# An adaptive-layer-norm block with windowed attention: w_mod's first third in two groups of feature columns, with the first Q weights between them

## The chip, the cores and the metric

The kernel runs on one core of one Trainium2 chip. The metric is the device time of one execution in microseconds, the median of several runs. The kernel before takes 323.13 us (three runs, 322.71 to 323.54).

## The reference, cut to what matters

`x` has 2048 rows of 640 features in bf16. Six modulation vectors of 640 come from one row `c` and `w_mod` (640 x 3840). The first third of `w_mod`'s columns gives `sa` and `ca`, with which the first layer norm's output is shifted and scaled before the QKV projection.

```python
mod = (_silu(c) @ w_mod).reshape(c.shape[0], 6, 1, -1)
sa, ca, ga, sb, cb, gb = ...
h = _layernorm(x, axis=-1) * (1 + ca) + sa
x = x + ga * _A_ref(h, A_wqkv, A_wo)        # 32 heads of 20, causal window of 256
h = _layernorm(x, axis=-1) * (1 + cb) + sb
x = x + gb * _B_ref(h, B_w_gate, B_w_up, B_w_down)   # (sigmoid(g) * u) @ w_down, F = 1536
```

## The kernel before

The 2048 rows are worked through in 8 chunks `a` of 256 rows, each two blocks `bi` of 128. For each chunk: layer norm (`ln1`, `ln_stats`), turning the normalized rows so that features lie on partitions (`hT`, five feature tiles `dt` of 128, called `kt` where they are summed over), modulation of `hT` by the columns `scA` and `shA`, projection to Q, K and V (`qkv`), attention (`score_set`, exponentials on ScalarE, masks on GpSimd, `burst` for the product with V, `norm`), output projection and MLP. TensorE works on chunks ahead: the projections of chunk a + 2 are issued before attention of chunk a.

**The order of work** is not decided at run time. `Prog.op` collects 2139 operations with their reads and writes; the list `PRIO` gives each a number. Sorted by it, the numbers give the order; the number modulo 5 names the engine (PE, ACT, DVE, POOL, SP). `schedule` only chooses buffers and semaphores along that order; `emit` writes each engine's instructions in it, with a wait wherever a read or write depends on another engine. So each engine works through its own list strictly, and a step whose input is late holds up all behind it on that engine. SP issues nearly all DMAs, in the order of its list, and they share one queue.

**The start** is what the change touches. Before anything can be projected, the modulation of layer norm one has to be known, so these come first:

- SP issues x block 0 (`load_x`), then w_mod's first third as six DMAs with an x block between: four by `load_bulk` (line 642), each one row tile `kt` of 128 rows x 1280 columns (320 KiB, runs of 2560 bytes), and the fifth row tile in two halves (lines 644 to 646). They lie for now in the space of `wd`. Then come wqkv's columns in pieces of 320 (`load_w3`, line 636, 400 KiB each, runs of 640 bytes): the first half of Q (`wq`), half of K, x blocks 2 and 3, the other half of K, V (640 columns), and the other half of Q.
- TensorE meanwhile runs six pairs of dummy products (`warm`, line 672), turns c, and seeds the sums with a product of the identity and a tile of ones (line 749), which adds the 1 of `1 + ca`.
- For each row tile of w_mod that has landed, TensorE runs ten products of 128x128 weights by a 128x64 tile of silu(c) repeated (`fnA`): five column groups `cg` of 128 for `ca` (bank 1) and five for `sa` (bank 0), summed over the five row tiles in two banks of `psA`. Behind the first three stand two padding products each (`pad`, line 682, from `FILL`).
- When all are summed, one VectorE copy (line 764) takes the ten columns to `mA`, whose halves are `shA` and `scA`.
- `pe_transposes` turns chunk 0: TensorE multiplies the normalized blocks by the identity (tag `aptr0`), three feature tiles in one bank and two in another; ScalarE or VectorE copies them to `hT` (line 838). Then ten modulations in place, one for each feature tile and block (lines 847 and 848), each of which waits for `R_mA`, that is for the whole copy.
- `qkv(0)` projects, 320 columns at a time, with five products over `kt` each. In the table before, the first Q columns of both blocks come first, then K's first. Their results go to `stg` (line 908 on ScalarE, 909 on VectorE), are turned by TensorE (`qtr0`) and copied to `QT` and `KT`. The first scores (`score0`) need these; two exponentials (line 1019) follow each score.

Lines 672, 682, 692 and 693 are helpers through which all of TensorE's products go. From chunk 1 on, the modulation is part of the copy (line 872/873) or follows a DMA transpose (line 815).

Of the kernel before, what the change touches and what calls it, by code (L numbers as in the profile page):

```python
# [361 lines left out]
def c_pe(n):  # L362
# [132 lines left out]
MW = 64  # L495
LEAD = 2
NE = 5
EW = 48 * 64
EDGE = 2
DEDGE = 0.245  # L500
FILL = (2, 2, 2, 0, 0)
WSE = (("dve", "pool"), ("dve", "pool"))
QMAX = 4.5
PAIR = 0
PAIRO = 0
XHP = ((2, 0), (3, 0), (4, 0), (4, 1), (5, 0), (5, 1))
OWE = lambda a: "sp"
# [3 lines left out]
def build(nc, A_x, A_wqkv, A_wo, B_x, B_w_gate, B_w_up, B_w_down, c, w_mod, out, S=2048):  # L511
# [61 lines left out]
    def R(name):  # L573
        return Res(name)
# [61 lines left out]
    def load_w3(lo, hi, work, prio, tag, **kw):  # L636
        dma(lambda: wqkv[:, :, lo:hi], lambda: wqkv_src[:, :, lo:hi], work, writes=R_w3[lo // 160:hi // 160], prio=prio, tag=tag, **kw)
# [653 lines left out]
```

## Time and profile before

| | before |
|---|---|
| median of 3 runs | 323.13 us (322.71 to 323.54) |
| profiled execution, its own time | 323.24 us |
| its span, first to last instruction | 321.5 us |
| granted TensorE clock | 1.000 |
| instructions | 11632 |
| DMA moved in the span | 37.85 MB |

The profile is one execution. Engines are PE (TensorE's products), PEld (its weight loads), DVE (VectorE), ACT (ScalarE), POOL (GpSimd) and SP, which only issues DMAs here. A busy time counts instructions only, not waits. An arrow back from a group or a row names what ended the wait before it. A row of the timeline has start, length, engine, line, operation and how many instructions were merged. A product's length contains the time in which it drains, so products that follow one another overlap: their pitch is what they cost.

### The profile page before, as it was taken

What the parts mean: (1) busy time and instruction counts of PE and PEld (TensorE: products, weight loads), DVE (VectorE), ACT (ScalarE), POOL (GpSimd) and SP (SyncE); (2) the same over time, 40 slices, a digit from 0 to 9 for tenths busy, and PEclk for the clock granted to TensorE, in tenths of its full rate; (3) what the DMA queues carried; (4) which work ended last, traced back from release to release, by engine and by line L of the source; (5) the groups of instructions that cost most, each with busy time, mean ns of one, the idle gap of its engine ahead of it and who ended that gap; (6) DMA issues with size and microseconds to landing.
All of it is one profiled execution on the core that took longest, in us unless ns stands there. A gap on an engine that the chain in (4) does not pass through costs nothing.

```text
span 321.5 us, 11632 instructions
## 1 busy us (share of the span) xinstructions
PE 316.9 (99%) x4877; PEld 223.9 (70%) x4877; DVE 209.7 (65%) x429; ACT 213.0 (66%) x315; POOL 178.4 (55%) x271
## 2 busy tenths in 40 slices
PE   8899999999999999999999999999999999999997
PEld 3565655557876677757776667887887788887885
DVE  4699997768779788764668457557472775454332
ACT  3599997989796869778867686877585753211120
POOL 4157987977666776887466576755647373002100
DMA  6999988899591728734027482240023112203101
GB/s 214 372 349 351 275 161 149 183 123 281 174 194 49 116 84 132 95 61 114 7 65 105 92 155 68 56 90 12 2 68 90 46 41 63 80 25 63 41 2 61
DMA packets 71182, 37.85 MB, mean 118 GB/s; under 512 B 45274, under 2 KB 69338, under 8 KB 71130
## 3 DMA queue, kind: packets, MB, share of 16 engines
q1 hardware_dynamic: 69968, 35.80, 48.3%
q10 hardware_dynamic: 1162, 1.31, 1.2%
q8 instruction: 38, 0.62, 0.9%
q14 instruction: 14, 0.11, 0.1%
HBM read 21.30 MB, written 5.25 MB: 83 GB/s over the span
## 4 chain that ended last, share of the span: by engine, by line
PE 96%; DMA 2%; SPq 1%; issue 0%; DVE 0%
PE M L692 80%; PE S L693 8%; PE M L693 7%; DMA wqkv<-in_A_wqkv_dram 2%; SPq L588 1%; DVE x L1215 0%
## 5 line engine op out<-in xcount | busy, mean ns | idle before, releaser
L1019 ACT ACTIVATE E<-S 128x512 bf16<-128x512 f32 (+2 forms) x184 | 150.7, 878 | 41.5 <-PE S L693 38.1
L1044 POOL TENSOR_SCALAR_AFFINE_SELECT E<-E 128x512 bf16<-128x512 bf16 (+1 forms) x176 | 139.5, 819 | 55.1 <-ACT E L1019 28.1
L692 PE MATMUL M<-wqkv,hT 128*128 128x480 bf16 (+1 forms) x340 | 73.6, 355 | 0.8 <-DMA wqkv<-in_A_wqkv_dram 0.8
L692 PE MATMUL M<-h2T,wu 128*128 128x256 bf16 x480 | 65.2, 273 | 0.0
L692 PE MATMUL M<-h2T,wg 128*128 128x256 bf16 x480 | 64.4, 273 | 0.0
L1196 DVE SCALAR_TENSOR_TENSOR hh<-sig,M 128x512 bf16<-128x512 f32 x48 | 32.7, 682 | 43.3 <-ACT sig L1194 32.4
L692 PE MATMUL M<-wd,hh 128*128 128x320 bf16 (+2 forms) x396 | 56.1, 295 | 0.0
L1194 ACT ACTIVATE sig<-M 128x512 f32<-128x512 f32 x48 | 28.8, 603 | 36.8 <-PE M L692 35.6
L692 PEld LDWEIGHTS M<-h2T,wg 128*128 128x128 bf16 x480 | 46.2, 98 | 6.9
L692 PEld LDWEIGHTS M<-h2T,wu 128*128 128x128 bf16 x480 | 45.3, 98 | 7.5 <-ACT E L1019 0.3
L692 PEld LDWEIGHTS M<-wqkv,hT 128*128 128x128 bf16 x340 | 30.3, 98 | 27.0 <-DMA wqkv<-in_A_wqkv_dram 0.9
L692 PEld LDWEIGHTS M<-wd,hh 128*128 128x128 bf16 x396 | 37.0, 98 | 15.0 <-issue 0.3
L693 PEld LDWEIGHTS S<-QT,KT 20*64 20x64 bf16 (+1 forms) x1856 | 19.9, 100 | 19.7 <-ACT E L1019 8.4
L693 PE MATMUL S<-QT,KT 20*64 20x256 bf16 (+5 forms) x1856 | 32.1, 228 | 0.0
L1215 DVE TENSOR_TENSOR x<-M,x 128x320 bf16<-128x320 f32 (+2 forms) x33 | 15.5, 475 | 23.1 <-PE M L692 22.7
L778 DVE BATCH_NORM_STATS2 st<-x 128x6 f32<-128x320 bf16 x64 | 28.7, 477 | 2.6 <-DMA x<-in_A_x_dram 2.1
L784 POOL TENSOR_SCALAR st<-st 128x2 f32<-128x2 f32 (+1 forms) x17 | 3.9, 229 | 42.3 <-DVE st L780 40.4
L1088 DVE STREAM_TRANSPOSE T<-M 128x512 f32<-128x512 f32 x32 | 21.6, 697 | 7.2 <-PE M L693 7.0
L692 PE MATMUL M<-wo,oT 128*128 128x320 bf16 x160 | 25.6, 300 | 0.0
L1149 DVE TENSOR_TENSOR x<-M,x 128x320 bf16<-128x320 f32 x32 | 15.5, 487 | 11.3 <-PE M L692 10.5
L693 PE MATMUL M<-E,V 128*32 128x128 bf16 (+1 forms) x960 | 22.8, 246 | 0.0
L693 PEld LDWEIGHTS M<-E,V 128*32 128x32 bf16 x960 | 19.1, 97 | 3.8 <-issue 1.7
(77 smaller groups left out, 239.1 us busy)
## 6 DMA issues: line engine op xcount, KB each, us to landing
x<-in_A_x_dram SPq DMA_DIRECT2D x24, 160.0 KB
doc<-On SPq DMA_DIRECT2D x64, 40.0 KB
wd<-in_B_w_down_dram SPq DMA_DIRECT2D x4, 480.0 KB
wqkv<-in_A_wqkv_dram SPq DMA_DIRECT2D x4, 400.0 KB
wu<-in_w_mod_dram SPq DMA_DIRECT2D x5, 320.0 KB
oT<-doc SPq DMA_DIRECT2D x8, 192.0 KB
out_dram<-x SPq DMA_DIRECT2D x9, 160.0 KB
wd<-in_w_mod_dram SPq DMA_DIRECT2D x4, 320.0 KB
```

Source lines behind the costliest of these rows:

```text
L588: return e.dma_start(dst(), src())
L692: return e.matmul(o, l, r, start=st, stop=sp, skip_group_check=True)
L693: return e.matmul(o, l, r, start=st, stop=sp, tile_position=tp, skip_group_check=True)
L778: A("dve", lambda e, g, bi=bi, j=j: e.bn_stats(v(bi * 12 + j * 6, 6), src[bi].ap[:, j * 320:(j + 1) * 320]), 0.48, reads=[src[bi].r()], wr ...
L784: A("pool", lambda e, g, lo=lo, hi=hi: e.tensor_scalar(v(28 + lo, hi - lo), var()[:, lo:hi], EPS, None, op0=ALU.add), 0.2, reads=[st.r(("m ...
L1019: A("act", lambda e, eng: e.activation(dst(), src(), ACT.Exp, scale=SM_SCALE), c_act(n), reads=[Sp.r()], writes=[E.r(key)], prio=3, tag=f" ...
L1044: A("pool", lambda e, eng: e.affine_select(rows(dst), rows(src), pattern=[[0, 8], [sign, n]], compare_op=ALU.is_ge, fill=0.0, base=base, c ...
L1088: A("dve", lambda e, g, h=h: e.transpose(T1.ap[:, 512 * h:512 * h + 512], X[h].ap), 0.694, reads=[X[h].r()], writes=[T1.r(h)], prio=3.5, t ...
L1149: A("dve", lambda e, g, ps=ps, bi=bi, half=half: e.tensor_tensor(x1[bi].ap[:, half * 320:half * 320 + 320], ps.ap[:, 0:320], x1[bi].ap[:, ...
L1194: A("act", lambda e, g, pg=pg, sg=sg: e.activation(sg.ap[:], pg.ap[:], ACT.Tanh, scale=0.5), c_act(512), reads=[pg.r()], writes=[sg.r()], ...
L1196: A("dve", lambda e, g, pu=pu, sg=sg, f0=f0: e.scalar_tensor_tensor(out=hh.ap[:, f0:f0 + 2, :], in0=sg.ap[:].rearrange("p (a b) -> p a b", ...
L1215: A("dve", lambda e, g, ps=ps, bi=bi, c0=c0, n=n: e.tensor_tensor(x1[bi].ap[:, c0:c0 + n], ps.ap[:, 0:n], x1[bi].ap[:, c0:c0 + n], op=ALU. ...
```

## The change

w_mod's first third is loaded, multiplied and copied in two groups of feature columns. Group A is feature tiles 0 to 2 (`SPL = 3`): 384 columns for `sa` and 384 for `ca`, in five DMAs, one for each row tile (192 KiB, runs of 768 bytes). Group B is feature tiles 3 and 4: 256 columns each, in three DMAs (row tiles 0 to 3 for `ca`, the same for `sa`, and row tile 4 for both; 256, 256 and 128 KiB, runs of 512 bytes). The first piece of Q's weights is cut in two: rows of feature tiles 0 to 2 (240 KiB) and of 3 and 4 (160 KiB).

```diff
-    load_bulk(wm_ap[0][:, 0:4, :], wm_src[:, 0:4, 0:1280], Rm[0][0:4], 1.1, 0.2, "wm0", cuts=(1, 2, 3, 4), lat=0.8)
...
+    SPL = 3
+    parts = [(0, SPL, kt, kt + 1, (1, 0)) for kt in range(NDT)] + [(SPL, NDT, 0, 4, (1,)), (SPL, NDT, 0, 4, (0,)), (SPL, NDT, 4, 5, (1, 0))]
...
+    for i, q in enumerate(parts):
+        c0, c1, k0, k1, banks = q
+        dma(lambda q=q: part(wm_ap[0], *q), lambda q=q: part(wm_src, *q),
+            0.11 * len(banks) * (c1 - c0) * (k1 - k0), writes=[R_part[i]], prio=0.2 + 0.01 * i, tag="wmA" if c0 == 0 else "wmB", lat=0.8)
...
-        load_w3(320 * i, 320 * i + 320, 1.05, 0.30 + 0.005 * i, "wq" if i < 2 else "wk", lat=0.9)
+        load_w3(320 * i, 320 * i + 320, 1.05, 0.30 + 0.005 * i, "wq" if i < 2 else "wk", parts=((0, SPL), (SPL, NDT)) if i == 0 else ((0, NDT),), lat=0.9)
...
+    for k, n in ((0, SPL), (1, NDT - SPL)):
+        psA_one.append(A("pe", lambda e, g, k=k, n=n: mm(e, psA.ap[:, k, 0:2 * n * MW], ident[:], Eall[:, 1, (SPL - n) * MW:(SPL + n) * MW], True, False), 0.16,
+                         reads=[R_one, R_ident], writes=[psA.r(k > 0)], prio=0, lat=0.2, tag="one", ni=2))
...
+    for i, (c0, c1, k0, k1, banks) in enumerate(parts):
+        def fnA(e, g, c0=c0, c1=c1, k0=k0, k1=k1, banks=banks):
+            for kt in range(k0, k1):
+                for bank in banks:
+                    for cg in range(c0, c1):
+                        ins = mm(e, place(c0, bank, cg),
+                                 wm_ap[0][:, kt, bank * D + cg * 128:bank * D + cg * 128 + 128], silubc[:, kt, 0:MW],
+                                 False, kt == NDT - 1)
+            return pad(e, FILL[k0]) if c0 == 0 and FILL[k0] else ins
...
+    for c0, c1 in ((0, SPL), (SPL, NDT)):
+        A("dve", lambda e, g, c0=c0, c1=c1: e.tensor_copy(mA[:, :, c0:c1], psA.ap[:, c0 > 0, 0:2 * (c1 - c0) * MW].rearrange("p (b a m) -> p b a m", b=2, m=MW)[:, :, :, 0]), 0.18,
+          reads=[psA.r(c0 > 0)], writes=[R_mA[c0 > 0]], prio=0, tag=f"fac{c0}")
...
-                    A(MOE, mo, {"dve": 0.24, "act": 0.48, "pool": 0.45}, port=True, reads=[dst.r(("t", dt, bi))] + Rmod,
+                    A(MOE, mo, {"dve": 0.24, "act": 0.48, "pool": 0.45}, port=True, reads=[dst.r(("t", dt, bi)), Rmod[dt >= SPL]],
...
-FILL = (2, 2, 2, 0, 0)
+FILL = (2, 1, 0, 0, 0)
```

Each group is seeded by a product of its own, with a tile of zeros (for `sa`) beside ones (for `ca`), and has its own bank. There are two copies to `mA`, and a modulation of chunk 0 waits only for the copy that holds its feature tile; `R_w3` likewise says of each Q piece which rows have landed. `PRIO` is a new table of 2147 numbers. In the start it reads, engine by engine:

- SP: x0, group A's row tile 2, x1, row tiles 1, 0, 4, 3, Q's first weights (rows of tiles 0 to 2), group B (`ca`, row tile 4, `sa`), Q's rest, K's first half, x3, x2, and on as before but for some pieces of w_mod's second third and x blocks.
- TensorE: group A's products, with the turning of block 0 among them and of block 1 behind, B's `ca` products, Q of block 0 over tile 0, then over tiles 1 and 2, B's `sa` products and row tile 4, Q of block 1 over tiles 0 to 2, then Q of both blocks over tiles 3 and 4, then K. In K, block 0's five products stand together, then a turn of Q, then block 1's.
- VectorE: both layer-norm statistics before both normalizations; the first copy, five modulations, the second copy, four modulations. POOL does the tenth; ScalarE none (two before). Three of the later evacuations change between ScalarE and VectorE.

From about 22 us on, every engine's list is the same as before.

More of the change, by code (lines that the diff above doesn't have):

```diff
@@ L574, in R @@
         return Res(name)
-    R_w3 = [R(f"wqkv{i}") for i in range(12)]
+    R_w3 = [[R(f"wqkv{i}a"), R(f"wqkv{i}b")] for i in range(12)]
     R_crow, R_ident, R_ccol, R_cth, R_siluc, R_silubc, R_wo = (R(n) for n in ("crow", "ident", "ccol", "cth", "siluc", "silubc", "wo"))
@@ L634, in build, with load_w3 @@
     wqkv_src = A_wqkv.rearrange("(t p) f -> p t f", p=128)
-    def load_w3(lo, hi, work, prio, tag, **kw):
-        dma(lambda: wqkv[:, :, lo:hi], lambda: wqkv_src[:, :, lo:hi], work, writes=R_w3[lo // 160:hi // 160], prio=prio, tag=tag, **kw)
+    def load_w3(lo, hi, work, prio, tag, parts=((0, NDT),), **kw):
+        for t0, t1 in parts:
+            dma(lambda t0=t0, t1=t1: wqkv[:, t0:t1, lo:hi], lambda t0=t0, t1=t1: wqkv_src[:, t0:t1, lo:hi], work * (t1 - t0) / NDT,
+                writes=[r for rs in R_w3[lo // 160:hi // 160] for r, t in zip(rs, (0, SPL)) if t0 <= t < t1], prio=prio, tag=tag, **kw)
     x0 = {}
@@ L747, in build @@
     R_one = R("one")
-    A("pool", lambda e, g: e.memset(Eall[:, 1, 0:5 * MW], 1.0), 0.3, writes=[R_one], prio=0)
-    p_E.init[1].append(A("pe", lambda e, g: mm(e, psA.ap[:, 1, 0:5 * MW], ident[:], Eall[:, 1, 0:5 * MW], True, False), 0.14,
-                         reads=[R_one, R_ident], writes=[psA.r()], prio=0, lat=0.2, tag="modA", ni=2))
+    A("pool", lambda e, g: e.memset(Eall[:, 1, 0:SPL * MW], 0.0), 0.25, writes=[R_one], prio=0, tag="ones")
+    A("pool", lambda e, g: e.memset(Eall[:, 1, SPL * MW:2 * SPL * MW], 1.0), 0.25, writes=[R_one], prio=0, tag="ones")
@@ new lines, in place @@
+    def place(c0, bank, cg):
+        at = bank * (SPL if c0 == 0 else NDT - SPL) * MW + (cg - c0) * MW
+        return psA.ap[:, c0 > 0, at:at + MW]
+    psA_one = []
+    for k, n in ((0, SPL), (1, NDT - SPL)):
+        psA_one.append(A("pe", lambda e, g, k=k, n=n: mm(e, psA.ap[:, k, 0:2 * n * MW], ident[:], Eall[:, 1, (SPL - n) * MW:(SPL + n) * MW], True, False), 0.16,
+                         reads=[R_one, R_ident], writes=[psA.r(k > 0)], prio=0, lat=0.2, tag="one", ni=2))
+    p_E.init[1].extend(psA_one)
@@ L751, in build @@
     oA = []
     fills = []
-    for kt, banks in [(kt, (1, 0)) for kt in range(NDT - 1)] + [(NDT - 1, (1,)), (NDT - 1, (0,))]:
-        def fnA(e, g, kt=kt, banks=banks):
-            for bank in banks:
-                for cg in range(5):
-                    ins = mm(e, psA.ap[:, bank, cg * MW:cg * MW + MW],
-                             wm_ap[0][:, kt, bank * D + cg * 128:bank * D + cg * 128 + 128], silubc[:, kt, 0:MW],
-                             kt == 0 and cg == 0 and bank == 0, kt == NDT - 1)
-            return pad(e, FILL[kt]) if FILL[kt] else ins
-        oA.append(A("pe", fnA, MW / 2400.0 * 5 * len(banks) + 0.2154 * FILL[kt], reads=[Rm[0][kt] if kt < NDT - 1 else R_half[banks[0]], R_silubc],
-                    writes=[psA.r()], prio=0, lat=0.2, tag="modA", ni=10 * len(banks) + 2 * FILL[kt], extra=wprev))
+    for i, (c0, c1, k0, k1, banks) in enumerate(parts):
[7 more added lines that the diff above has]
+            return pad(e, FILL[k0]) if c0 == 0 and FILL[k0] else ins
+        nf = FILL[k0] if c0 == 0 else 0
+        np = len(banks) * (c1 - c0) * (k1 - k0)
+        oA.append(A("pe", fnA, MW / 2400.0 * np + 0.2154 * nf, reads=[R_part[i], R_silubc],
+                    writes=[psA.r(c0 > 0)], prio=0, lat=0.2, tag="modA" if c0 == 0 else "modB", ni=2 * np + 2 * nf, extra=wprev + [psA_one[c0 > 0]]))
@@ L898, in ln1 @@
         if a < NPH:
-            turned[a] = pe_transposes(src, t, scA, shA, [R_mA], 1, a)
+            turned[a] = pe_transposes(src, t, scA, shA, R_mA, 1, a)
         else:
@@ L936, in qkv @@
             name = "q" if lo < D else "k" if lo < 2 * D else "v"
-            pe_chain(ps, wid, pairs, [R_w3[lo // 160:hi // 160] + [hT[a].r((kt, bi))] for kt in range(NDT)], prio, f"proj{name}{a}", hold=hold, first=a == 0 and hi <= 2 * D)
+            pe_chain(ps, wid, pairs, [[rs[kt >= SPL] for rs in R_w3[lo // 160:hi // 160]] + [hT[a].r((kt, bi))] for kt in range(NDT)], prio, f"proj{name}{a}", hold=hold, first=a == 0 and hi <= 2 * D)
             m = min(hi, 2 * D)
```

15 lines of the change are left out of this document (7 added, 8 removed), and 225 rows, old and new, of the table PRIO.

## The prediction

> **What bounds the kernel now.** I read the page first (busy time by engine, then the chain that ended last), then the chain in order of time, then the first 25 us in the timeline and in windows of 1 us. From the page:
>
> ```profile
> span 321.5 us, 11632 instructions
> PE 316.9 (99%) x4877; PEld 223.9 (70%) x4877; DVE 209.7 (65%) x429; ACT 213.0 (66%) x315; POOL 178.4 (55%) x271
> PE 96%; DMA 2%; SPq 1%; issue 0%; DVE 0%
> ```
>
> TensorE is busy 316.9 of 321.5 us and carries 96% of the chain. All it could win back is 4.6 us, part of which is the start and the last store. The 2% of DMA is one piece, at the head of the chain in order of time. The list of waits has it too, and two windows place it:
>
> ```profile
> 4.76 6.30 DMA wqkv<-in_A_wqkv_dram
> PE M L692 <- DMA wqkv<-in_A_wqkv_dram: 0.8, 1, 0.8
> 10.29:11.10 0.81, 0.00 (x0) 0.00 (x0) 0.70 (x5) 0.57 (x3) 0.00 (x0) 1.00 1.13 377
> 11.10:13.10 2.00, 1.99 (x13) 0.97 (x14) 1.82 (x9) 0.90 (x3) 0.00 (x0) 1.00 1.11 374
> ```
>
> In a window row the first column is the length, then the busy time of PE, PEld, DVE, ACT and POOL, the granted clock, the DMA share and GB/s. So the first Q weights land at 4.76 + 6.30 = 11.06 us, TensorE is empty from 10.29 to 11.10, and from there it is full. DMA runs at full stretch in that gap (377 GB/s): the start is bound by bytes. The change therefore matters by when the first projection ends and what stands behind it. The rest of the kernel only moves with that point.
>
> The stages of the start, from the timeline (start, length, engine, line; xN merges N):
>
> ```profile
> 2.17 2.54 SPq L588 DMA_DIRECT2D wd<-in_w_mod_dram  x5
> 4.76 1.42 SPq L588 DMA_DIRECT2D wqkv<-in_A_wqkv_dram  x2
> 7.88 3.38 SPq L588 DMA_DIRECT2D wqkv<-in_A_wqkv_dram  x3
> 7.04 0.46 PE L692 MATMUL S<-silubc,wd 128*128 128x64 bf16 x10
> 8.78 0.60 PE L682 MATMUL S<-E 128*128 128x512 bf16 x2
> 9.07 0.47 PEld L692 LDWEIGHTS S<-silubc,wd 128*128 128x128 bf16 x10 [0.20 <-DMA wd<-in_w_mod_dram]
> 9.78 0.51 PE L692 MATMUL S<-silubc,wd 128*128 128x64 bf16 x10
> 10.34 0.16 DVE L764 COPY mA<-S 128x10 f32<-128x10 f32 x1
> 10.60 0.88 ACT L847 ACTIVATE hT<-hT,mA 128x128 bf16<-128x128 bf16 x2 [0.24 <-DVE mA L764]
> 10.61 1.87 DVE L848 TENSOR_SCALAR hT<-hT,mA 128x128 bf16<-128x128 bf16 x8
> 11.11 2.69 PE L692 MATMUL M<-wqkv,hT 128*128 128x320 bf16 x16 [0.82 <-DMA wqkv<-in_A_wqkv_dram]
> ```
>
> Read downwards: w_mod's products, the copy to `mA`, ten modulations of `hT`, then projections. The last modulation ends at 10.61 + 1.87 = 12.48, so the first ten Q products are held by the modulations almost as much as by the weights. Of the 16 products in the last row ten are Q's and six K's; I call the first of K's K0. When K0 starts follows from the pitch of products that wait for nothing:
>
> ```profile
> 14.42 1.11 PE L692 MATMUL M<-wqkv,hT 128*128 128x320 bf16 x7
> L692 PE MATMUL M<-wqkv,hT 128*128 128x320 bf16 x16 | 2.7, 300 | 0.8 <-DMA wqkv<-in_A_wqkv_dram 0.8
> 13.63 0.95 PE L692 MATMUL M<-ident,stg 128*128 128x128 bf16 x12
> 12.35 0.44 ACT L908 ACTIVATE stg<-M 128x320 bf16<-128x320 f32 x1 [0.88 <-PE M L692]
> 14.06 0.60 ACT L908 ACTIVATE QT<-M 128x512 bf16<-128x512 f32 x1
> 15.47 0.40 PE L693 MATMUL S<-QT,KT 20*128 20x256 bf16 x8
> 15.92 1.94 ACT L1019 ACTIVATE E<-S 128x1024 bf16<-128x1024 f32 x2 [0.32 <-PE S L693]
> 18.36 1.94 ACT L1019 ACTIVATE E<-S 128x1024 bf16<-128x1024 f32 x2
> 20.44 0.40 PE L693 MATMUL S<-QT,KT 20*128 20x128 bf16 x16
> ```
>
> Seven products take 1.11 us and one 0.30, so the pitch is (1.11 - 0.30)/6 = 0.135. K0 starts six products before the end of the row of 16: 13.80 - 0.30 - 5 x 0.135 = 12.82. Twelve transposes take 0.95 with their waits. From 15.47 to 20.44 it goes score, two exponentials (1.94), score, two exponentials (1.94, to 20.30), score: there ScalarE sets the pace, and when the first score starts decides when TensorE gets through this stretch.
>
> **The change part by part.** The order tables, old and new, give each engine's order. From about 22 us on all five are the same as before (the last 878 of 929 TensorE steps, 387 of 429 VectorE, 307 of 323 ScalarE), so all that can move the time lies in the start.
>
> *Bytes.* The amount is unchanged; the order is not. Before: x block 0 and 1 (320 KiB), w_mod (1600), wq's first 320 columns (400): w_mod ends at 1920 KiB, the weights at 2320. After: both x blocks and group A (960, together 1280), wq's rows 0 to 383 (240, at 1520), group B (640, at 2160), wq's rest (160, at 2320), then K's first 400 (2720). So the first weights come 800 KiB earlier in the stream, but the last byte of w_mod comes 240 KiB later. Rates, by windows of 1 us:
>
> ```profile
> 3.00:4.00 1.00, 1.00 (x4) 0.38 (x4) 0.87 (x3) 0.00 (x0) 0.00 (x0) 1.00 1.12 328
> 4.00:5.00 1.00, 1.00 (x4) 0.45 (x3) 0.26 (x3) 0.21 (x1) 0.57 (x2) 1.00 0.76 246
> 5.00:6.00 1.00, 1.00 (x3) 0.30 (x2) 0.72 (x3) 0.16 (x1) 0.46 (x2) 1.00 0.76 207
> 6.00:7.00 1.00, 1.00 (x9) 0.63 (x8) 0.97 (x4) 0.40 (x2) 0.28 (x2) 1.00 0.82 291
> 7.00:8.00 1.00, 1.00 (x22) 0.72 (x21) 0.40 (x3) 0.68 (x2) 0.74 (x2) 1.00 0.99 375
> 9.00:10.00 1.00, 1.00 (x23) 0.88 (x22) 0.13 (x1) 0.02 (x1) 0.00 (x0) 1.00 1.12 362
> 17.00:18.00 1.00, 1.00 (x14) 0.58 (x15) 1.00 (x3) 0.88 (x2) 1.00 (x7) 1.00 1.04 401
> ```
>
> The wait that ended at 9.07 is for w_mod's fourth row tile, 1600 KiB into the stream; the weights at 2320 KiB landed at 11.06. That is 720 KiB in 2.0 us, 365 GB/s, so w_mod ended at about 9.95. Counted back at 375, 1280 KiB stand at 9.07 - 0.87 = 8.20. Forward at 365: wq's first part +0.67, group B (655 KB) +1.80: group B ends at 10.67.
>
> *Smaller pieces.* Group A moves in runs of 768 B, group B in runs of 512 B, w_mod before in runs of 2560 and 1280 B. No row shows those two sizes. The nearest: 375 GB/s at 7 to 8 us, where w_mod's long runs dominate, against 362 at 9 to 10, where wqkv's 640 B runs come in, 3.5% less. Bounds for the rate of B: 401 (17 to 18 us, best) to 207 (5 to 6 us, worst, with the share only 0.76); rows with the share above 1 give 328 at worst. I take group A 3.5% longer (0.09) and B's rate at 355 (0.05), both nearest to the 640 B row: L, the landing of group B, is **10.8** (10.5 at 401 and no loss on A; 11.0 at 328; 12.1 at 207).
>
> The Trainium skill (DMA: Bandwidth & Descriptors, "Why small descriptors are slow (HBM only)") states about 3 cycles of fixed cost for a packet beside one cycle for each 32 bytes. As an estimate from that page, 83 cycles for 2560 B become 27 for each 768 B, 8% a byte, and B's runs cost 3% more than 640 B ones: L would be about 10.95 and the sum 0.15 us higher. The trace goes the same way but less steeply, 3.5% from mostly long runs to mostly 640 B.
>
> *From L to K0.* The products of w_mod:
>
> ```profile
> L692 PE MATMUL S<-silubc,wd 128*128 128x64 bf16 x50 | 2.3, 193 | 0.0
> L682 PE MATMUL S<-E 128*128 128x512 bf16 x7 | 2.2, 379 | 0.0
> ```
>
> The first row gives a pitch of (0.46 - 0.19)/9 = 0.03, the second, padding, (0.60 - 0.38) = 0.22. Before, the copy starts 10.34 - 9.95 = 0.39 after the landing, with the last five products. After, TensorE meets B's last DMA in its queue first (8 products) and then the third part (4): 12 instead of 5, 7 x 0.03 = 0.2 more. Copy at L + 0.59, first modulation 0.27 later as before (10.61 - 10.34). Before, eight modulations on VectorE and two on ScalarE follow; after, only the four of feature tiles 3 and 4, all on VectorE: pitch (1.87 - 0.31)/7 = 0.223, so the last ends at L + 0.59 + 0.27 + 0.67 + 0.31 = L + 1.84. The other six Q products are done by then: they need the first copy, whose products end by about 9.4 (TensorE starts group A when its third piece, at 896 KiB, lands: 8.20 - 393 KB/375 = 7.2; from there 30 products at 0.03, 3 paddings at 0.22 and 8 transposes in some 0.6), and five modulations at 0.223 on VectorE: to 10.9, before L. The last Q pair runs at L + 1.9, K0 at L + 2.16 = **12.96, against 12.82**. So the six products taken off the path (6 x 0.135 = 0.8 us) do not pay: group B comes 0.85 us after the old end of w_mod, and its 1.8 us tail of copy, modulation and two products is nearly the old one. K's weights land at L + 573 KB/365 = L + 1.57, 0.6 before K0: no new wait there.
>
> *From K0 to the first score.* Old order: score after 13 K products and 12 transposes. New order: after 15 and 12, and on ScalarE the evacuations run k, QT, k, QT one after the other. ScalarE: the k half after K0 + 0.88, 0.44; QT 0.57; k 0.42; QT 0.60; so the score can start at K0 + 2.94 = 15.90, while TensorE is ready at K0 + 15 x 0.135 + some 0.8 = K0 + 2.8. A K evacuation that moves from VectorE to ScalarE (0.44) fits between that score and its exponentials, 15.47 to 15.92 before. Before it started at 15.47: **+0.43**. The exponentials behind it fill ScalarE to 20.4, so the delay stays; at best TensorE's own +0.14 is what remains, at worst L = 11.0 gives +0.65.
>
> *What costs nothing, and its cover.* Three more DMA issues (two from w_mod, one from wq) on the sync queue, each 0.5 us (2.54/5): the queue issues Q's weights 6.3 us before they land and later issues stretch to 1.1 us each (3.38/3) without harm, so they hide; uncovered, x blocks 2 and 3 and the later weights come 1.5 us later. Some pieces of w_mod's second third and x blocks change places on that queue; they are used from 22 us on; uncovered, one piece of 320 KiB is 0.9 us. One more bias product and a second memset: 0.3 us in the warm-up of dummy matmuls; uncovered 0.3. Padding in these products falls from 6 to 3 matmuls of 0.22: 0.65 us less in a stretch that waits for DMA. The product of group B now stands in TensorE's queue ahead of the first Q products: up to 0.4 us in which they wait though their weights are there, covered by the wait for L; without that cover, 0.4. One modulation goes to POOL, at most 0.56 us:
>
> ```profile
> L815 POOL TENSOR_SCALAR hT<-hT,mA 128x256 bf16<-128x256 bf16 x9 | 4.9, 555 | 1.3 <-DVE hT L815 1.2
> 14.67 0.23 POOL L784 TENSOR_SCALAR st<-st 128x2 f32<-128x2 f32 x1 [6.84 <-DVE st L780]
> ```
>
> The row is for twice its width; behind it on POOL is only the next layer norm, at 14.67 after 6.84 us of idling. Uncovered, it delays the Q product that reads it by 0.55.
>
> *Sum.* Bytes and copies to K0 +0.14, ScalarE's order to the score +0.29, the rest +0: +0.43. The profiled execution took 323.24 us (span 321.5), 0.11 over the median of 323.13: 323.67 against it, **323.6** for a median. A measurement here can tell about 0.3% (1.0 us) from no change, so this is no change by that bound.
>
> **The rivals.**
>
> (1) *Hidden anyway.* L is 10.5, so K0 is at 12.66 and the score at 15.60 (+0.13), or ScalarE keeps TensorE's pace (-0.16): 323.1. For it: TensorE is full from 11.1 on, ScalarE is only 45% busy in 11.1 to 13.1. Against: only the best rate of any row gives that L.
>
> (2) *The early slump of the stream goes away* (the other direction). Between 4 and 7 us DMA moves 246, 207 and 291 GB/s although eight issues stand in the queue; at 365 it would have moved 0.35 MB more, worth 1.0 us. If shorter runs spread better, everything lands 1.0 us earlier: 322.1 to 322.6. Decides if the 5 to 6 us row rises above 300. Against: nothing in the change touches what else is going on there.
>
> (3) *Short runs are slow.* If 512 B runs move at the worst rate of a row, 207, L is 12.1 and the time 323.6 + 1.3 = 324.9. It passes 0.3% once B's rate is under about 280 (L at 11.3). For it: only rows with a share under 1 are that slow; the next worst is 328.
>
> (4) *The clock.* Padding is halved and TensorE idles in three places. The warm-up ran at half pace:
>
> ```profile
> 4.34 2.37 PE L672 MATMUL S<-E 128*128 128x512 bf16 x6
> ```
>
> That is (2.37 - 0.38)/5 = 0.40 a product, against 0.22 for the same product as padding later: half pace from the start of the warm-up to about 6 us, some 4.7 us. One such spell near 12 us costs half of it, 2.35: 326.0. Against: the 0.81 us gap at 10.29 left the pitch at 0.135. The Trainium skill (TensorE: Matmul & The Clock Gate, "What's actually happening") has the clock drop after an idle window of about 3.4 us; the longest gap I expect is 0.5, so by it rival 4 stays away, and the trace agrees as far as 0.81 us goes.
>
> **How the numbers follow.** Forecast (+0.1 to +0.85) 0.50, rival 1 0.20, rival 2 0.08, rival 3 0.15, rival 4 0.07. Faster by over 0.3%: rival 2, 0.08. Slower: 3 and 4, 0.22. Same: 0.70. The forecast's own range is 323.2 to 324.0. The range for 8 in 10 leaves out rivals 2 and 4 and takes in rival 3 (324.9) and, below, rival 1 (323.1) less the 0.4 by which the lowest run (322.71) lies under the median: 322.7 to 325.0.
>
> **What would show it.** The first Q product near 10.2 instead of 11.1; a second copy to `mA` near 11.4; K0 near 12.96; the first score near 15.9 with TensorE idle just before it; the third score at 20.9 instead of 20.44; the same order and the same idle time from 22 us on. I am wrong if group B lands before 10.3, if the products after 11 us step at 0.27, or if the difference arises after 22 us.

## The result, and the profile after

The changed kernel takes 324.22 us (median of 11 runs, 323.90 to 324.68) against 323.54 us for the kernel before, measured beside it. The ratio is 1.0025, with a 95% interval of 1.0016 to 1.0033. In a second series it was 1.0026 (1.0013 to 1.0039). So the change makes the kernel slower by some 0.7 us, under the 0.3% that I took as the limit of what a measurement can tell from no change; the intervals, which exclude 1, show that with this many runs less can be told. The profiled execution took 324.01 us. One run of the kernel before (401 us) and one of r2 below (529 us) had granted clocks of 0.755 and 0.56 and stand in no ratio.

The page of the kernel after, its span, its busy times and the shares of the chain:

```profile
span 322.2 us, 11634 instructions
PE 315.7 (98%) x4875; PEld 223.1 (69%) x4875; DVE 209.5 (65%) x429; ACT 212.9 (66%) x315; POOL 178.9 (56%) x273
PE 93%; SPq 3%; DMA 3%; issue 0%; DVE 0%
```

TensorE is busy 1.2 us less (316.9 before), and the span is 0.7 us longer, so TensorE idles 1.9 us more. Three padding products fewer are 0.65 of the busy time. The warm-up is shorter too: its last four products (4.80 to 5.83 us) step at 0.22 us, where six stepped at 0.40 before, so TensorE came to full pace earlier in this execution.

The start, from the timeline of the kernel after (start, length, engine, line; xN merges N):

```profile
6.88 0.35 PE L702 MATMUL S<-silubc,wd 128*128 128x64 bf16 x6 [1.05 <-DMA wd<-in_w_mod_dram]
9.11 0.17 DVE L786 COPY mA<-S 128x6 f32<-128x6 f32 x1 [1.12 <-PE S L702]
9.76 0.41 PE L702 MATMUL S<-silubc,wd 128*128 128x64 bf16 x8 [0.52 <-DMA wd<-in_w_mod_dram]
10.00 0.30 PE L702 MATMUL M<-wqkv,hT 128*128 128x320 bf16 x1
10.96 0.52 PE L702 MATMUL S<-silubc,wd 128*128 128x64 bf16 x12 [0.28 <-DMA wd<-in_w_mod_dram]
11.52 0.16 DVE L786 COPY mA<-S 128x4 f32<-128x4 f32 x1 [0.80 <-PE S L702]
11.79 0.98 DVE L870 TENSOR_SCALAR hT<-hT,mA 128x128 bf16<-128x128 bf16 x4
12.47 1.48 PE L702 MATMUL M<-wqkv,hT 128*128 128x320 bf16 x9 [0.59 <-DVE hT L870]
14.32 0.59 ACT L930 ACTIVATE QT<-M 128x512 bf16<-128x512 f32 x1
15.12 0.69 DVE L931 CAST KT<-M 128x512 bf16<-128x512 f32 x1 [0.27 <-PE M L702]
15.34 0.60 ACT L930 ACTIVATE QT<-M 128x512 bf16<-128x512 f32 x1
16.05 0.15 PEld L703 LDWEIGHTS S<-QT,KT 20*128 20x128 bf16 x8 [0.40 <-DVE KT L931]
16.08 0.40 PE L703 MATMUL S<-QT,KT 20*128 20x256 bf16 x8
16.53 1.94 ACT L1041 ACTIVATE E<-S 128x1024 bf16<-128x1024 f32 x2
21.16 0.40 PE L703 MATMUL S<-QT,KT 20*128 20x128 bf16 x16
```

The first Q product now runs at 10.00 instead of 11.11, as meant. But the single wait of 0.81 us before has become four: 1.05, 0.52, 0.28 and 0.59 us. The last two are the price of the split: group B's last piece lands just before 10.96, and the four modulations behind the second copy hold the last four Q products until 12.47 and beyond. K0 is the fifth product before the end of the row of nine: 12.47 + 1.48 - 0.30 - 4 x 0.136 = 13.11, against 12.82. The first score starts at 16.08, against 15.47, behind two `QT` copies on ScalarE. The row of its weight load names VectorE's `KT` copy, but that ended at 15.81, and ScalarE's second `QT` copy at 15.94. Five profiles tell the two apart: the score starts 0.14 us behind the end of that `QT` copy in both profiles of after, in r2, r3 and r9, and 0.09 to 0.27 us behind the `KT` copy's. So ScalarE's copy is what it waits for.

The chain of the kernel after in order of time, its longest piece (start, length, what):

```profile
10.60 8.72 DMA wqkv<-in_A_wqkv_dram
```

The last Q weights land at 10.60 + 8.72 = 19.32 (17.52 before), and TensorE starts their products only at 19.36. That adds 0.1 us: the shift against before is 0.61 us at the first score, 0.72 at the third (21.16 against 20.44) and 0.74 at the end. From the third score on it stays within 0.02 us.

### The profile page after: what moved, and what is told of

Same layout as the page of the kernel before. It is cut to its first block, busy times and chain, and to the rows that moved or that the text cites. A ratio compares the mean times of both kernels' runs of the same rounds, so it can differ in the third digit from the quotient of the medians.

```text
span 322.2 us, 11634 instructions
## 1 busy us (share of the span) xinstructions
PE 315.7 (98%) x4875; PEld 223.1 (69%) x4875; DVE 209.5 (65%) x429; ACT 212.9 (66%) x315; POOL 178.9 (56%) x273
## 4 chain that ended last, share of the span: by engine, by line
PE 93%; SPq 3%; DMA 3%; issue 0%; DVE 0%
PE M L702 78%; PE S L703 8%; PE M L703 7%; SPq L589 3%; DMA wqkv<-in_A_wqkv_dram 3%; DVE x L1237 0%
## 5 line engine op out<-in xcount | busy, mean ns | idle before, releaser
L1237 DVE TENSOR_TENSOR x<-M,x 128x320 bf16<-128x320 f32 (+2 forms) x33 | 15.5, 475 | 22.8 <-PE M L702 22.4
L1171 DVE TENSOR_TENSOR x<-M,x 128x320 bf16<-128x320 f32 x32 | 15.5, 487 | 11.6 <-PE M L702 10.5
```

Of the source, the lines that this page charges most:

```text
L1171: A("dve", lambda e, g, ps=ps, bi=bi, half=half: e.tensor_tensor(x1[bi].ap[:, half * 320:half * 320 + 320], ps.ap[:, 0:320], x1[bi].ap[:, ...
L1237: A("dve", lambda e, g, ps=ps, bi=bi, c0=c0, n=n: e.tensor_tensor(x1[bi].ap[:, c0:c0 + n], ps.ap[:, 0:n], x1[bi].ap[:, c0:c0 + n], op=ALU. ...
```

## The experiments

The steps are called by their tags: `projq0`, `projk0` and `projv0` are the products, `qtr0` the turns, `evqk0` the evacuations to `stg`, `evqt0` the copies to `QT` and `KT`, `astats1` the statistics of layer norm of chunk 1, `wmA`/`mA` and `wmB`/`mB` DMAs and products of the groups (`mB_03` row tiles 0 to 3, `mB_4` the fifth). Where only the order of a list is edited, the diff shows the list.

| kernel | median us | ratio to before (95%) | K0 | first score | score - K0 |
|---|---|---|---|---|---|
| before, profile | 323.24 (one) | | 12.82 | 15.47 | 2.65 |
| after, profile | 324.22 | 1.0025 (1.0016 to 1.0033) | 13.11 | 16.08 | 2.97 |
| after_again | 324.03 | 1.0026 (1.0013 to 1.0039) | 13.11 | 16.07 | 2.97 |
| r1_oldtail | 324.04 | 1.0012 (1.0003 to 1.0022) | 13.38 | 16.30 | 2.91 |
| r2_newtail | 323.72 | 1.0004 (0.9994 to 1.0013) | 12.72 | 15.69 | 2.97 |
| r3_bfirst | 324.30 | 1.0011 (0.9997 to 1.0025) | 12.69 | 15.67 | 2.98 |
| r4_bfirst_oldtail | 323.94 | 1.0006 (0.9997 to 1.0016) | 12.49 | 15.53 | 3.04 |
| r5_spread | 323.42 | 0.9995 (0.9987 to 1.0004) | 12.26 | 14.93 | 2.67 |
| r5_again | 323.57 | 1.0009 (0.9996 to 1.0021) | 12.58 | 15.23 | 2.65 |
| r6_qtfix | 324.74 | 1.0038 (1.0026 to 1.0050) | 12.78 | 15.44 | 2.66 |
| r7_longruns | 323.90 | 1.0021 (1.0010 to 1.0033) | 13.31 | 15.96 | 2.65 |
| r8_runs640 | 324.58 | 1.0039 (1.0025 to 1.0053) | 15.44 | 18.40 | 2.96 |
| r9_afterspread | 324.03 | 1.0018 (1.0008 to 1.0028) | 13.01 | 15.98 | 2.97 |
| r10_runs1280 | 325.83 | 1.0060 (1.0041 to 1.0078) | 14.56 | 18.62 | 4.06 |

K0 and first score are from the profiled execution of each, in us. Medians are over all runs, 11 or 12 of each kernel, 5 of r6. The median of before beside them was 323.52 to 323.55. The profiles of r8 and r10 hold a spell at half the TensorE clock between Q's first products and the first score (last section). By their granted clock of 0.995, three of r8's twelve runs and seven of r10's have it; the medians of the others are 324.37 and 324.12 us.

### Theory and rivals

My theory: two things delay the first score by about equal parts. Group B ends later than all of w_mod did, with its tail of copy, modulations and products behind it (K0); and the new order from K0 to the score has ScalarE do four copies one after the other. Rival: the small pieces slow the stream. A second rival came from the first profiles: late weights, by one slow part of a transfer, set the time whatever the order.

### Undo the tail, and do it alone

```diff
 order behind the last Q pair, after -> r1 (before -> r2 is the reverse)
-PE   projk0#0 #1 #2, qtr0#0, projk0#6 #7 #8, qtr0#2, qtr0#4, projk0#9 #10 #11, score0#0
+PE   projk0#0 #1 #2 #6, qtr0#4, qtr0#0, qtr0#2, projk0#7 #8 #9 #10, score0#0
-ACT  evqk0#0 #4 #2, evqt0#0, evqk0#6, evqt0#4, evqk0#7, exp0#1
+ACT  evqk0#0 #4 #2, evqt0#4, evqt0#2, evqk0#6, exp0#0
-DVE  astats1..., evqt0#2, axh1#1, axh1#0, evqk0#3
+DVE  astats1..., evqt0#0, axh1#1, axh1#0, evqk0#7, evqk0#3
```

> The changed kernel up to the last pair of Q products; behind it every engine's list in the order of the kernel before. Theory (the late second group costs 0.3 us up to the first K product, the new order of K, its turns and ScalarE's evacuations another 0.3 up to the first score): the first K product stays at 13.1, the first score comes at 15.75 instead of 16.08, the time is 0.3 to 0.45 us over the kernel before. Rival (TensorE is full from there on, so the order behind the first K product is worth nothing and all of the loss is made ahead of it): 0.6 to 0.8 over before, like the changed kernel.

> The kernel before up to the last pair of Q products; behind it the order of the changed kernel. Theory: the first K product stays at 12.8, the first score comes at 15.8 instead of 15.47, 0.3 to 0.45 us over the kernel before. Rival (order behind the first K product worth nothing): no difference from before, within 0.1.

The timeline of r2, with only the new tail:

```profile
11.00 2.56 PE L690 MATMUL M<-wqkv,hT 128*128 128x320 bf16 x15 [0.81 <-DMA wqkv<-in_A_wqkv_dram]
15.69 0.40 PE L691 MATMUL S<-QT,KT 20*128 20x256 bf16 x8
```

The row has Q's ten products and K's first five, so K0 is at 11.00 + 2.56 - 0.30 - 4 x 0.136 = 12.72 and the score 2.97 later. The last column of the table says the same of all kernels in which nothing else was late: 2.65 to 2.67 in the old order (before, both r5, r6, r7), 2.97 or 2.98 in the new (both profiles of after, r2, r3, r9). The tail costs 0.32 us at the first score. In the times it shows less: r2's ratio is 1.0004, not told from 1 and under the 0.3 to 0.45 us that were expected, while r1, with 1.0012, has half of the change's ratio, as expected. r1's own profile missed its expected score (16.30 instead of 15.75) twice over: group B landed 0.27 us later than in after (11.18), and with it K0, and K's second weights landed at 15.74 instead of 14.49, so that the wait hid what the order gave.

### Group B first

```diff
 SP
-wmA3, wq#0a, wmB_03b1, wmB_4, wmB_03b0, wq#0b
+wmA3, wmB_03b1, wmB_4, wmB_03b0, wq#0a, wq#0b
 PE
-mB_03b1, projq0#0, aptr0#3, projq0#1, mB_03b0, mB_4, projq0#6
+mB_03b1, aptr0#3, mB_03b0, mB_4, projq0#0, projq0#1, projq0#6
 r4 also has the old order behind the last Q pair, as r1
```

> The changed kernel with one thing undone: the second group of w_mod is loaded and multiplied before Q's first weights, both groups still in their own pieces and with their own copies. Theory (what decides is when w_mod's last byte lands): it lands near 10.2 instead of 10.9, the last modulation ends near 12.0, the first K product starts at 12.5 where K's weights land, the first score near 15.5; 0.0 to 0.2 us over before. Rival (the small pieces slow the stream, and the place of the group is indifferent): the weights behind land as late as in the changed kernel and the time stays 0.5 or more over before.

> Both undone: second group before Q's weights, and the order of the kernel before behind the last pair of Q products; what is left of the change are the groups themselves. Theory: the two terms add up, first K product 12.5, first score 15.15, 0.2 to 0.4 us under the kernel before. Rival (small pieces): at or above before, 0 to 0.3.

Timelines of r3, first two rows, and of r4:

```profile
15.67 0.40 PE L700 MATMUL S<-QT,KT 20*128 20x256 bf16 x8
20.06 1.53 PE L699 MATMUL M<-wqkv,hT 128*128 128x320 bf16 x10 [1.00 <-DMA wqkv<-in_A_wqkv_dram]
```

```profile
10.91 2.57 PE L699 MATMUL M<-wqkv,hT 128*128 128x320 bf16 x16 [0.18 <-DMA wqkv<-in_A_wqkv_dram]
15.53 0.40 PE L700 MATMUL S<-QT,KT 20*128 20x256 bf16 x8 [0.31 <-DVE QT L928]
18.31 0.85 PE L699 MATMUL M<-wqkv,hT 128*128 128x320 bf16 x5 [0.96 <-DMA wqkv<-in_A_wqkv_dram]
```

With group B first, its last piece lands at 10.17 and the first score comes 0.41 us earlier than in after (r3), near the 15.5 that was expected: the place of Q's weights in the stream is what delays K0. r3's time doesn't show it: its median, 324.30, is no lower than after's, and its ratio of 1.0011 can be told neither from 1 nor from after's. And r4, with both parts undone, was expected 0.2 to 0.4 us faster than before and is not faster, as its rival has it. Its profile shows two things in place of the gain: a `QT` copy on VectorE that stands behind the statistics of x blocks which land at 12.88 and 13.34 (0.31 us of waiting), and weights that land late (0.96 us; 1.00 in r3's). A start that is made shorter in one place meets the next late input.

### Free the QT copy

```diff
 r4 -> r6
-PE   projk0#0 #1 #2 #6, qtr0#4, qtr0#0 ... aptr1#4, qtr0#6, projv0#4, projv0#5
+PE   projk0#0 #1 #2, qtr0#0, projk0#6, qtr0#4 ... qtr0#6, projv0#4, projv0#5, aptr1#4
-DVE  astats1#4, astats1#3, astats1#0, ..., evqt0#0
+DVE  astats1#4, astats1#3, evqt0#0, astats1#0, ...
```

> As r4_bfirst_oldtail (group B loaded and multiplied before Q's weights, order of the kernel before behind), but the first QT copy on VectorE stands ahead of the statistics of x block 2, the turn of Q ahead of K's second five products, and chunk 1's turning moves behind six of V's products. Theory: r4's first score (15.53) was held by that copy behind the statistics, which wait for late x blocks; without it the first score comes near 15.2 and the time is 0.2 us less than before (ratio 0.9994), 0.4 less than r4. Rival: late weights, by the landing of one slow transfer behind 14 us, set the time in all of these kernels; then the first score may come early, TensorE waits again for wk, wv or wq before 20 us, and the median is that of r4 (ratio 1.0005 or more).

```profile
15.44 0.40 PE L700 MATMUL S<-QT,KT 20*128 20x256 bf16 x8
18.13 0.28 PE L699 MATMUL M<-ident,x 128*128 128x128 bf16 x2 [0.28 <-DVE stg L928]
19.66 1.52 PE L699 MATMUL M<-wqkv,hT 128*128 128x320 bf16 x10 [0.26 <-DVE hT L892]
```

Both theories missed. From K0 to the score it is 2.66 again, so the copy is free; but K0 stands at 12.78, since K's weights land at 12.73. And what was pushed behind on VectorE, chunk 1's layer norm, is late next: TensorE waits twice for VectorE, and the third score comes at 21.45 instead of 20.44. TensorE waited for no weights behind 14 us here. VectorE's order in this stretch has no slack either.

### One modulation from VectorE to ScalarE

```diff
 before -> r5
-ACT  amodu0#1, amodu0#6        DVE  amodu0#0 #2 #5 #4 #3 #7 #9 #8
+ACT  amodu0#1, amodu0#3, amodu0#6        DVE  amodu0#0 #2 #5 #4 #7 #9 #8
 after -> r9
-DVE  fac3, amodu0#3 #4 #8 #9
+DVE  fac3, amodu0#3 #8 #9        ACT  amodu0#4
```

> The kernel before with one edit: of the ten modulations of chunk 0, one more goes from VectorE to ScalarE (seven and three instead of eight and two). Theory: in the kernel before, the first Q products are held by the modulations as much as by the weights, and the head of the chain is modulation, K, ScalarE's copies, first score. Then the last modulation ends near 12.25 us instead of 12.48, K0 starts near 12.6 instead of 12.82, the first score near 15.25 instead of 15.47, and the time is 0.2 us less than before (ratio 0.9994). Rival: the weights and the x blocks, by their landing, set the first score whatever the modulations do; then it stays at 15.4 to 15.5 and the time at 1.000.

> The kernel before with one more modulation on ScalarE, once more. Theory: the first time 0.34 us of the profile's gain were a faster stream (Q's weights landed at 10.72 instead of 11.06) and 0.2 the modulation; so the distance from the landing of Q's weights to K0 is again 1.55 us (1.76 before), and the ratio 0.999 to 1.000. Rival: no gain that holds, ratio 1.000 or above.

> The changed kernel, with one of the four modulations behind the second copy on ScalarE instead of VectorE. Theory (the tail behind group B is copy, four modulations one after the other, last Q products): the last modulation ends 0.2 us earlier against group B's landing, K0 follows group B's landing by 2.0 us instead of 2.2, the first score comes 0.2 earlier (15.8 to 15.9), and the time is 0.2 us less than the changed kernel's (ratio to before 1.0015 to 1.002). Rival (ScalarE's four copies between K and the first score set it): the modulation delays the first of them or leaves it in place, the first score stays at 16.0 to 16.1 and the ratio at 1.0025.

Timelines of r5, of its second run, and of r9:

```profile
10.77 2.47 PE L690 MATMUL M<-wqkv,hT 128*128 128x320 bf16 x16 [0.81 <-DMA wqkv<-in_A_wqkv_dram]
14.93 0.40 PE L691 MATMUL S<-QT,KT 20*128 20x256 bf16 x8
```

```profile
11.00 2.55 PE L690 MATMUL M<-wqkv,hT 128*128 128x320 bf16 x16 [0.79 <-DMA wqkv<-in_A_wqkv_dram]
15.23 0.40 PE L691 MATMUL S<-QT,KT 20*128 20x256 bf16 x8
```

```profile
12.47 1.38 PE L699 MATMUL M<-wqkv,hT 128*128 128x320 bf16 x9 [0.53 <-DVE hT L867]
15.98 0.40 PE L700 MATMUL S<-QT,KT 20*128 20x256 bf16 x8
19.36 1.53 PE L699 MATMUL M<-wqkv,hT 128*128 128x320 bf16 x10 [0.22 <-DMA wqkv<-in_A_wqkv_dram]
```

In the kernel before, ten Q products take 1.71 us up to K0; with the modulation moved, 1.49 and 1.58. So the modulations did hold Q, by 0.1 to 0.2 us. The rest of r5's first gain was a stream that came 0.34 us earlier in that profile (10.72; 10.89 the second time). The second time the distance from the landing of Q's weights to K0 was 1.69 us, not the 1.55 that was expected. Over both series no gain is to be told (0.9995 and 1.0009), as the rivals have it. In r9 the tail behind group B shrinks as the theory has it, by 0.15 us where 0.2 was expected: group B lands at 10.96, K0 follows 2.05 us later instead of 2.20, and the score keeps its 2.97. It comes at 15.98, 0.10 us earlier than in after and not at 15.8 to 15.9, since group B landed 0.05 us later. Late Q weights then ate the gain of that profile; the ratio of all runs, 1.0018, lies where it was expected, but its interval holds 1.0025 too.

### The changed kernel once more

> The changed kernel once more, beside the others. Theory (group B's landing and the order of ScalarE's copies): group B lands at 10.8 to 11.2, the first score at 16.0 to 16.3, and the ratio is 1.002 to 1.003. Rival (one late landing of wq made up the last 0.1 to 0.3 us of the profile after): TensorE does not wait before 20 us for wq, the shift from 21 us on is 0.3 to 0.6 instead of 0.72, and the ratio is 1.001 to 1.002.

```profile
9.76 0.41 PE L702 MATMUL S<-silubc,wd 128*128 128x64 bf16 x8 [0.24 <-DMA wd<-in_w_mod_dram]
12.46 1.48 PE L702 MATMUL M<-wqkv,hT 128*128 128x320 bf16 x9 [0.53 <-DVE hT L870]
16.07 0.40 PE L703 MATMUL S<-QT,KT 20*128 20x256 bf16 x8
20.99 0.40 PE L703 MATMUL S<-QT,KT 20*128 20x128 bf16 x16
```

Group B lands at 10.90, K0 and the score are those of the first profile to 0.01 us, and the end is 0.62 us later than before's, with no wait for late weights. So 0.6 us is the part that repeats. The rival was right on this shift and wrong on the ratio.

### The price of the pieces

```diff
 r4 -> r7: groups, copies and order of r4, DMAs of before
-    for i, q in enumerate(parts):
-        dma(lambda q=q: part(wm_ap[0], *q), lambda q=q: part(wm_src, *q), ...)
+    for kt in range(4):
+        dma(lambda kt=kt: wm_ap[0][:, kt, :], lambda kt=kt: wm_src[:, kt, 0:1280], ...)
+    for i in (1, 0):
+        dma(lambda i=i: wm_ap[0][:, 4, i * D:i * D + D], lambda i=i: wm_src[:, 4, i * D:i * D + D], ...)
```

```diff
 before -> r8 (RUN = 320) and r10 (RUN = 640): each of the first four row tiles in two DMAs
-    load_bulk(wm_ap[0][:, 0:4, :], wm_src[:, 0:4, 0:1280], Rm[0][0:4], ..., cuts=(1, 2, 3, 4))
+    def cols(ap, i):
+        return ap.rearrange("p (a i f) -> p a i f", i=2, f=RUN)[:, :, i, :]
+    for k in range(4):
+        for i in range(2):
+            dma(lambda k=k, i=i: cols(wm_ap[0][:, k, :], i), lambda k=k, i=i: cols(wm_src[:, k, 0:1280], i), ...)
```

> As r4_bfirst_oldtail (two groups of products and two copies, same order), but w_mod's first third is loaded as in the kernel before: four row tiles of 1280 columns in runs of 2560 bytes and the fifth in two halves, not in runs of 768 and 512 bytes. This is the price of the small pieces by itself. Theory: w_mod's last piece lands near 9.9 us instead of 10.17, the first score comes near 15.3 to 15.5, and the time is 0.1 to 0.3 us less than r4's (ratio about 1.0000). Rival: the size of the runs does not matter, the stream's rate is set by what else moves; then w_mod ends at 10.1 to 10.2 again and the time is r4's, 1.0006.

> The kernel before, all its order kept, but each of the first four row tiles of w_mod's first third moves in two DMAs of alternate groups of 320 columns, so in runs of 640 bytes instead of 2560. Products wait for both. This measures short runs by themselves, without groups, without moved weights. Theory (short runs are slower: in the profiles so far w_mod's last byte, 1920 KiB into the stream, lands at 9.55 to 9.95 us with long runs and at 10.17 to 10.50 with runs of 768 and 512 bytes): w_mod ends at 10.1 to 10.4, Q's weights land at 11.2 to 11.6, the time is 0.3 to 0.5 us more than before (ratio 1.001 to 1.0015). Rival (run to run chance): w_mod ends at 9.6 to 9.95, ratio 1.000.

> As r8_runs640, with the same count of DMAs, but each of them takes 640 adjoining columns: runs of 1280 bytes. Theory (the size of the runs counts, not the count of DMAs): w_mod ends 0.2 to 0.4 us before r8's, at 9.7 to 10.0, and the ratio is 1.000 to 1.0005. Rival (four more DMAs cost by themselves): as r8.

The timeline of r7:

```profile
9.68 0.33 PE L702 MATMUL S<-silubc,wd 128*128 128x64 bf16 x6 [0.63 <-DMA wd<-in_w_mod_dram]
11.04 0.28 PE L702 MATMUL S<-ident,x 128*128 128x128 bf16 x2 [0.62 <-ACT hT L860]
15.96 0.40 PE L703 MATMUL S<-QT,KT 20*128 20x256 bf16 x8
```

With before's long runs w_mod ends at 9.55 us instead of r4's 10.17, earlier still than the 9.9 that was expected. The time doesn't follow (1.0021, with 1.0000 expected): group A then needs both halves of the fifth row tile, so its last products start at 9.68 and end by 10.0 instead of 8.96, and the turns behind them in TensorE's list, which wait for a copy in both kernels (0.62 us here, 0.54 in r4), run at 11.04 instead of 9.98. So K0 is later (13.31), not earlier. What the trace says of the stream over all kernels (time at which the DMA that ends 2320 KiB into the stream, Q's first weights, landed, from the DMA events; the first number is when eight of its sixteen parts had):

| w_mod's pieces | kernels | half landed | landed |
|---|---|---|---|
| 6 DMAs, runs of 2560 and 1280 B | before, r2, r5 twice, r7 | 9.66 to 10.15 | 10.63 to 11.06, mean 10.85 |
| 8 DMAs, runs of 768 and 512 B | after twice, r1, r3, r4, r6, r9 | 10.44 to 10.85 | 11.33 to 11.63, mean 11.47 |
| 10 DMAs, runs of 640 and 1280 B | r8 | 10.74 | 12.76 |
| 10 DMAs, runs of 1280 B | r10 | 10.69 | 12.68 |

The first two groups don't overlap, and kernels of both stand in each of the three series of experiments: the smaller pieces cost 0.6 us by the time that Q's weights are in. In r8 w_mod ended at 10.00, between what theory and rival had, and Q's weights came over a microsecond later than the 11.2 to 11.6 expected. In r10 fifteen of the sixteen parts of w_mod's last piece were in at 9.98 and the last at 11.54, with 9.7 to 10.0 expected. Both ratios lie above what was expected. So r10 speaks against my reading that the length of the run is what counts: with runs of 1280 bytes it is as late as r8. That is one profile of each, both of runs with the spell at half pace (r8's is its slowest, 326.17 us), so landings near 12.7 need not be typical of these kernels. Whether the length below 2560 bytes or the count of DMAs costs it stays open; no run here separates them. r8 and r10 show a second thing, below.

## Why the prediction was right or wrong, point by point

The time, 324.22 us, lies in the range (322.7 to 325.0), and no change by the 0.3% bound was the likeliest case. The predicted 323.6 is 0.6 us low, of which 0.4 is the base: over 11 runs the kernel before has a median of 323.54, not 323.13. The medians differ by 0.68 us, 0.47 were predicted. The forecast's condition reaches to +0.85, but the worst case that it works out is +0.65.

- *The first score*, the sum of the argument: +0.43 predicted, +0.61 and +0.60 measured. The mechanism holds; its terms:
- *L, the landing of group B*: 10.8 predicted, 10.91 and 10.90 measured. The mis-sized term is the price of smaller pieces: I put 0.09 + 0.05 us, and the table of landings gives about 0.6. The error showed as 0.1 only because the profile of before that I counted from had the latest Q weights of its kind (11.06, mean 10.85), and the two of after are among the earlier of theirs (11.33 and 11.37, mean 11.47). In this profile the price lay in group B alone: group A was in at 8.09, no later than the 8.20 that I counted from, and B's 640 KiB took from 8.84 to 10.91, 317 GB/s, not 355. The windows of after:

```profile
8.00:9.00 1.00, 1.00 (x28) 0.88 (x27) 0.00 (x0) 0.35 (x1) 0.00 (x0) 1.00 1.15 344
9.00:10.00 1.00, 0.48 (x15) 0.31 (x11) 0.79 (x4) 0.73 (x2) 0.00 (x0) 1.00 1.10 309
10.00:11.00 1.00, 0.72 (x13) 0.37 (x10) 0.72 (x3) 0.42 (x2) 0.80 (x2) 1.00 1.12 328
```

The share is 1.10 or more in each, so DMA was at full stretch and moved less (369, 362 and 369 GB/s in the same windows before). The Trainium skill (DMA: Bandwidth & Descriptors, "Why small descriptors are slow (HBM only)") had L at 10.95 as I worked it out from its fixed cost for a packet. That is nearer than my 10.8, and its sum 0.15 us higher nearer too. Its 3% between runs of 512 and 640 bytes is less than the 13% between the 365 GB/s that I took from before, where runs of 640 bytes are over half, and the 317 here, and r10, as late as r8 with runs twice as long, doesn't show what it says of the length.
- *From L to K0*: 2.16 predicted, 2.20 and 2.21 measured. Copy, four modulations and the last products do what their rows of before said, and r9 moved one of them, with 0.15 of the expected 0.2 us.
- *From K0 to the first score*: 2.94 predicted, 2.97 measured, 2.65 in the old order. This term carries half of the loss, and r2 shows it by itself. The order on ScalarE (k, `QT`, k, `QT`) starts at K0 + 0.88, as it was worked out. But the lengths written down add to 2.91, not 2.94; measured, the last `QT` copy ends at K0 + 2.83, and the score follows 0.14 later, for which the sum had nothing. So that this term comes out to 0.03 us is in part luck.
- *That the delay stays*: right. Up to the second score ScalarE's exponentials kept it: that score comes 2.44 us behind the first in both orders. From there TensorE's own list does: the third score, at 21.16 and 20.99 instead of the predicted 20.9, starts 0.32 us behind the four turns ahead of it, as it does before.
- *What costs nothing*: only three of the six Q products were done by L, not all six (10.00 and 10.24; the other three run at 11.31, behind group B's products). It cost nothing, since TensorE then waits 0.59 us for the modulations anyway. The modulation on POOL was in time. Not foreseen was the lateness of the second half of Q's weights, 19.32 instead of 17.52, worth 0.1 us in the profile. The prediction looked only at when DMAs are issued, not at their spread in landing.
- *The first Q product*: 10.2 predicted, 10.00 and 10.12 measured. The wait of 1.05 us at 6.88, for the row tile of group A that TensorE multiplies first, I had only as idling in a stretch that waits for DMA; that tile landed at 6.83, where the sum had 7.2.
- *Rival 1* needed group B at 10.5, and it landed at 10.91. *Rival 2*, the slump of the stream early on, needed over 300 GB/s at 5 to 6 us: it was 286 (207 before), so it was partly filled, but without a gain. *Rival 3*, 207 GB/s for B, is excluded by the 317. *Rival 4*, the clock, though the longest gap was 1.05 us and not 0.5, did not come in either profile (from K0 on the row of nine steps at 0.136, after a gap of 0.59 us), but it is real: one of 23 runs of the changed kernel has a granted clock of 0.995 and took 325.37 us, so have one of r3, two of r7 and three of r8, and r10 has it in most, see the last section.

## What to carry to other kernels

Splitting a transfer so that work can begin earlier pays only if the last byte that the *end* of the stage needs does not move back; here Q's weights went ahead of 640 KiB that the last Q products need, and finer pieces cost the stream 0.6 us. Count the last consumer, not the first. And where two or three engines are each within 0.3 us of being late, an order put together from parts of two may gain nothing (r4, r7) or be slower than either whole (r6).

## What the runs showed of the hardware that I had not expected

*Half pace after a short wait.* The timeline of r8, and its windows (length, busy time of PE, PEld, DVE, ACT, POOL, granted clock, DMA share, GB/s):

```profile
12.80 3.93 PE L698 MATMUL M<-wqkv,hT 128*128 128x320 bf16 x16 [2.43 <-DMA wqkv<-in_A_wqkv_dram]
```

```profile
12.00:13.00 1.00, 0.20 (x1) 0.18 (x2) 0.56 (x3) 0.00 (x0) 0.00 (x0) 0.82 1.10 369
13.00:14.00 1.00, 1.00 (x5) 0.60 (x4) 0.00 (x0) 0.00 (x0) 0.00 (x0) 0.50 1.10 301
14.00:15.00 1.00, 1.00 (x6) 0.55 (x4) 0.66 (x2) 0.38 (x1) 0.00 (x0) 0.50 0.99 356
15.00:16.00 1.00, 1.00 (x6) 0.54 (x5) 1.00 (x4) 0.37 (x2) 0.00 (x0) 0.50 1.05 371
16.00:17.00 1.00, 1.00 (x13) 0.85 (x11) 0.25 (x3) 0.49 (x3) 0.57 (x2) 0.97 1.18 385
```

The same of r10:

```profile
11.59 0.32 PE L698 MATMUL S<-silubc,wd 128*128 128x64 bf16 x5 [0.87 <-DMA wd<-in_w_mod_dram]
12.72 3.65 PE L698 MATMUL M<-wqkv,hT 128*128 128x320 bf16 x16 [0.81 <-DMA wqkv<-in_A_wqkv_dram]
```

```profile
14.00:15.00 1.00, 1.00 (x6) 0.57 (x5) 0.79 (x3) 0.60 (x2) 0.00 (x0) 0.64 0.92 321
15.00:16.00 1.00, 1.00 (x6) 0.56 (x4) 1.00 (x4) 0.24 (x1) 0.00 (x0) 0.50 1.03 367
16.00:17.00 1.00, 1.00 (x10) 0.89 (x9) 0.22 (x2) 0.60 (x2) 0.61 (x2) 0.50 1.12 371
17.00:18.00 1.00, 1.00 (x11) 0.81 (x9) 0.74 (x2) 0.74 (x2) 0.34 (x1) 0.65 1.07 379
```

Worked out from the clock column, half pace lasts 3.42 us in both: 0.36 + 3 + 0.06 in r8, 0.72 + 2 + 0.70 in r10. In r8 a wait of 2.43 us was enough; in r10 two of 0.87 and 0.81 with products between. The sum of the waits alone doesn't decide it: r1 waited 0.85, 0.31 and 0.58 us within 3.6 us (9.14 to 12.74), and its clock stayed at 1.000. Of r10's 12 runs the seven with a clock of 0.995 took 325.7 to 326.6 us, the five with 1.000 took 324.0 to 324.9: the spell costs nearly 2 us. The Trainium skill (TensorE: Matmul & The Clock Gate, "What's actually happening") has a free-running window of 3413 ns, which agrees with the 3.42; but that the clock drops after an idle window, read as one without products, doesn't: in the 3.42 us ahead of the drop, TensorE idled 2.3 us in r8 and only 1.5 in r10. The kernel after idles 1.4 us between 9.2 and 12.6 (0.52 + 0.28 + 0.59), which is close, and would explain its one run at 0.995; that is an argument, not a measurement.

*One part of a transfer comes late.* In r8 and r10 half of Q's weights had landed at 10.74 and 10.69, the last of the sixteen parts 2.0 us later; in the kernels of the first two groups of the table above the last part came 0.7 to 1.2 us after the half. TensorE's waits of 2.43 us (r8) and of 1.00 and 0.96 us (r3, r4), and the late Q weights of after, are of this kind. Why one part lags, the runs don't show. The traces have one packet of instructions of 16 KB, about 1.1 us long, at 15.5 to 17.2 us in every profile, and the lag of weights behind it grows in several. That it holds up the part in question wasn't tried, and it can't be the whole reason: in r1, r8 and r10 a part lags already ahead of it.
